# An attention and two-layer feed-forward kernel in which one softmax mask in sixteen goes to GpSimd, and the first keys are loaded ahead of tau

## The chip, the cores and the metric

The kernel runs on one core of a Trainium2 chip. The metric is the device time of one execution in microseconds (us). A core has a matmul engine (TensorE, in profiles PE, its weight loads PEld), VectorE (DVE), ScalarE (ACT), GpSimd (POOL) and SyncE (SP), which here only issues DMAs. Each engine runs its own instructions in order; semaphores tie the engines together.

## What is computed

The reference, cut to what matters. The attention output goes through two feed-forward blocks; q, k, v are (4, 8, 576, 64), tau is 0.02, the feed-forward blocks work on 2304 tokens of width 512 with 2048 hidden units.

```python
scores = scale * np.matmul(q, k.transpose(0, 1, 3, 2))
thresh = np.max(scores, axis=-1, keepdims=True) - tau
scores = np.where(scores >= thresh, scores, -1000000000.0)
scores = scores - np.max(scores, axis=-1, keepdims=True)
attn = np.exp(scores)
attn = attn / (np.sum(attn, axis=-1, keepdims=True) + 1e-09)
x = np.matmul(attn, v)             # heads put side by side: (2304, 512)
h = x @ w_in;  x = (h * (1.0 / (1.0 + np.exp(-1.702 * h)))) @ w_out
h = x @ w_in2; out = (h * np.tanh(np.log1p(np.exp(h)))) @ w_out2
```

So a softmax row keeps only the scores that lie within tau of the row's largest one.

## The kernel before, in words

**Attention stage.** The 4 x 8 heads are taken in 16 pairs. The 576 query rows of a pair make four "full" groups (128 rows of each of the two heads), and the last 64 rows of four heads make a "mix" group after every second pair: 64 + 8 = 72 groups, numbered gi = 0 to 71. A group's two halves (i = 0 and 1) each go through these steps:

- `qk` (L600): TensorE writes the scores into two PSUM tiles `sc`, four matmuls for a full group (L623).
- `softmax_a` (L632): VectorE scales the scores into an SBUF buffer (ring `ss`, which a profile shows under the name `win2a` of the memory that it borrows) and takes the row's extreme with it (L646); GpSimd adds tau to that extreme (L650, one column, tile `nm`); ScalarE makes the exponentials into a tile `p` (L653; in a profile `g0a` to `g3a`); VectorE zeroes those below the threshold and sums the rest, in one instruction of 577 columns (L656, a scalar_tensor_tensor with an accumulated sum).
- `turn` (L678): TensorE transposes `p` into PSUM banks `tb` 0 to 2 (L692, L697; nine instructions for a group), ScalarE copies them to SBUF (L712; in a profile `wout1a`, `wout2a`, and a short one in `g0a`, `g1a`).
- `product` (L720): for every second group TensorE multiplies with v into bank `tb` 3 (L735, ten instructions), ScalarE copies the result (L744). `product_mix` (L747, L760) does the same for mix groups. `finish` (L662) takes reciprocals of the sums.

Until the first transposes TensorE is filled with dummy transposes (`keep_warm`, L574).

**Feed-forward stages.** `weights` and `stage` bring weights through ScalarE, VectorE and GpSimd (`conv_w`, L409 to L423, and L476 to L499), `load_xs` the tokens; `hidden` (L848) makes the hidden units with a 7-product Strassen scheme (L862), `out1` and `out2` multiply them with the second weights (L937, L940, L982). Some of the weights' preparation is done by VectorE, ScalarE and GpSimd while the attention stage still runs.

**What sets the order.** Nothing is issued as the code is read. Every operation is recorded with `add` in a class `Order` (L75): its engine, an assumed duration, what it reads and writes, and a rank. `Order.run` then plays the operations against the assumed durations, picks on each engine the ready one of lowest rank, and issues them in that order. Operations marked `port=True` are planned so that VectorE and GpSimd don't run them at the same time. The table `NUDGE` moves the rank of single operations, which it names by their running number. The order of each engine is thus fixed when the program is built; on the chip each engine takes it in that order and waits where it must.

**Start.** `make_ident` (L787) builds the identity, issues the load of tau (L789) and sets constants, and VectorE works out two columns from tau (L798, L799). The keys and values of a head pair are loaded by `prep` (L593: L596 and L597).

## Time and profile before

| what | value |
|---|---|
| median of 2 runs | 1024.49 us (1024.36 to 1024.63) |
| profiled execution: its time | 1024.41 us |
| profiled execution: its span, first to last instruction or landed DMA | 1022.5 us |
| busy in the span: PE / DVE / ACT / POOL | 1016.1 / 829.7 / 659.1 / 166.0 us |
| granted TensorE clock, mean | 0.999 of full speed |

The span is the part that the trace shows; 1.9 us of the execution's time lie outside it. "Busy" is the union of an engine's instructions. An engine that is busy all the time need not set the time, and one that idles costs nothing unless another waits for it, so the waits and the start times are read beside the busy shares.

### The profile page before, as it was taken

The page shows a single profiled execution, that of the slowest core. Times are in us where ns is not written, and L with a number is a line of the kernel's source. Part 1 is how long each engine was busy: PE and PEld are TensorE (multiplying, and loading weights), DVE is VectorE, ACT ScalarE, POOL GpSimd, SP SyncE. Part 2 cuts the span into 40 slices and gives each one's busy share as a digit, 9 for nine tenths or more (in the row PEclk, how much of TensorE's full clock was granted, in tenths as well). Part 3 has the DMA queues.
Part 4 walks back from the last instruction along what each step waited for, and adds up shares of the span by engine and source line. Part 5 has one row for each costly group of instructions (what it writes and reads, how often), then busy time and mean ns, then how long its engine had stood idle before and what let it go on. Part 6 is the DMA issues. An engine that isn't in the chain of part 4 may idle for free.

```text
span 1022.5 us, 17345 instructions
## 1 busy us (share of the span) xinstructions
PE 1016.1 (99%) x6362; PEld 865.9 (85%) x6362; DVE 829.7 (81%) x1642; ACT 659.1 (64%) x1262; POOL 166.0 (16%) x182
## 2 busy tenths in 40 slices
PE   9999999999999999999999999999999999999998
PEld 6666666666899999999999999989989899889987
DVE  7999999999989898888888779865598575975643
ACT  5988888888976768766777667644464444544421
POOL 2333544323222211201121011000000000000000
PEclk9999999999999999999999999999999999999999
DMA  5443347432256538664475553511144211232001
GB/s 198 138 135 101 117 141 236 161 98 74 87 169 210 182 124 282 243 201 159 146 271 200 193 185 110 194 67 62 63 124 145 83 49 55 93 114 83 21 1 63
DMA packets 55366, 137.53 MB, mean 134 GB/s; under 512 B 8432, under 2 KB 18672, under 8 KB 55280
## 3 DMA queue, kind: packets, MB, share of 16 engines
q1 hardware_dynamic: 55280, 136.41, 39.7%
q8 instruction: 50, 0.82, 0.3%
q14 instruction: 36, 0.29, 0.1%
HBM read 105.38 MB, written 31.01 MB: 133 GB/s over the span
## 4 chain that ended last, share of the span: by engine, by line
PE 99%; DMA 0%; DVE 0%; ACT 0%; issue 0%; SPq 0%; ACTq 0%
PE h L862 34%; PE tb L982 13%; PE tb L937 13%; PE sc L623 8%; PE tb L735 8%; PE tb L697 7%; PE h L940 7%; PE h L982 6%; PE tb L692 1%; PE tb L760 1%; DMA win1a<-in_kq 0%; PE tb L574 0%; DVE x21b L1000 0%; ACT wout2a L712 0%; ACT wout1a L712 0%
## 5 line engine op out<-in xcount | busy, mean ns | idle before, releaser
L876 DVE TENSOR_TENSOR hs<-h,u 128x384 f32<-128x384 f32 x144 | 79.9, 555 | 82.5 <-PE h L862 44.9
L862 PE MATMUL h<-xq,win2b 128*128 128x384 f32 x672 | 131.2, 335 | 0.0
L862 PE MATMUL h<-xq,win 128*128 128x384 f32 x672 | 131.1, 336 | 0.0
L862 PE MATMUL h<-xq,win1b 128*128 128x384 f32 x672 | 131.0, 335 | 0.0
L884 ACT COPY u<-h 128x384 f32<-128x384 f32 x144 | 68.8, 478 | 83.6 <-PE h L862 82.7
L862 PEld LDWEIGHTS h<-xq,win2b 128*128 128x128 f32 x672 | 115.9, 188 | 5.4 <-ACT u L884 0.2
L862 PEld LDWEIGHTS h<-xq,win1b 128*128 128x128 f32 x672 | 116.0, 188 | 5.3
L862 PEld LDWEIGHTS h<-xq,win 128*128 128x128 f32 x672 | 115.5, 188 | 5.2 <-ACT u L884 0.3
L646 DVE TENSOR_SCALAR_CACHE_REDUCE win2a<-sc,nqsc 128x576 f32<-128x576 f32 x144 | 111.6, 810 | 5.1 <-PE sc L623 4.7
L879 ACT ACTIVATE hs<-hs 128x384 f32<-128x384 f32 x144 | 75.9, 527 | 60.4 <-DVE hs L876 59.3
L650 POOL TENSOR_SCALAR nm<-nm,tau_p 128x1 f32<-128x1 f32 x144 | 81.8, 569 | 160.8 <-DVE win2a L646 159.5
L623 PE MATMUL sc<-win1a 64*128 64x288 f32 (+3 forms) x672 | 89.9, 414 | 0.3 <-DMA win1a<-in_kq 0.3
L481 DVE TENSOR_TENSOR sv<-sv 128x256 f32<-128x256 f32 x192 | 82.2, 429 | 1.3
L421 POOL TENSOR_TENSOR sg<-sg,sr 128x1024 uint32<-128x1024 uint32 x16 | 40.9, 2558 | 213.9 <-DVE sg L418 94.4
L623 PEld LDWEIGHTS sc<-win1a 64*128 64x128 f32 (+1 forms) x672 | 50.6, 173 | 26.1 <-issue 8.3
L476 ACT CAST win1b<-sv 128x256 fp32r<-128x256 f32 (+1 forms) x96 | 42.2, 445 | 33.9 <-DVE sv L481 28.9
L476 ACT CAST win2b<-sv 128x256 fp32r<-128x256 f32 (+1 forms) x96 | 42.3, 443 | 33.0 <-DVE sv L481 24.6
L476 ACT CAST win<-sv 128x256 fp32r<-128x256 f32 (+1 forms) x96 | 42.2, 446 | 27.5 <-DVE sv L481 21.7
L477 DVE TENSOR_TENSOR win2b<-sv,win2b 128x256 fp32r<-128x256 f32 (+1 forms) x96 | 50.6, 532 | 9.8 <-ACT win2b L476 9.6
L421 POOL TENSOR_TENSOR sv<-sv,sr 128x1024 uint32<-128x1024 uint32 x16 | 42.7, 2671 | 78.7 <-DVE sv L418 27.3
L477 DVE TENSOR_TENSOR win1b<-sv,win1b 128x256 fp32r<-128x256 f32 (+1 forms) x96 | 45.6, 478 | 10.1 <-ACT win1b L476 9.9
L477 DVE TENSOR_TENSOR win<-sv,win 128x256 fp32r<-128x256 f32 (+1 forms) x96 | 46.3, 486 | 7.2 <-ACT win L476 6.9
(244 smaller groups left out, 2285.7 us busy)
## 6 DMA issues: line engine op xcount, KB each, us to landing
sv<-w_d SPq DMA_DIRECT2D x80, 512.0 KB
sr<-in_w_in SPq DMA_DIRECT2D x16, 1024.0 KB
sr<-in_w_out SPq DMA_DIRECT2D x32, 512.0 KB
win1a<-in_kq SPq DMA_DIRECT2D x16, 576.0 KB
xr<-x_d SPq DMA_DIRECT2D x24, 384.0 KB
w_d<-sv SPq DMA_DIRECT2D x16, 512.0 KB
w_d<-sg SPq DMA_DIRECT2D x16, 512.0 KB
x_d<-xo SPq DMA_DIRECT2D x16, 288.0 KB
```

What stands on the lines that cost most here:

```text
L421: lambda: nc.gpsimd.tensor_tensor(bits, bits, word(0), ALU.add), keys, [kval], rank, port=True)
L476: add("ACT", t_act(256 * m, psum=False), lambda: nc.scalar.copy(at(0), src), [ku] + pre_in, keys, rank)
L477: add("DVE", t_dve(256 * m), lambda: nc.vector.tensor_tensor(at(1), src, at(0), ALU.subtract), [ku], keys, rank, port=True)
L481: add("DVE", t_dve(256), lambda: nc.vector.tensor_tensor(out, x, y, op), [], [ku], rank, port=True)
L623: nc.tensor.matmul(sc[i][at:at + m, g, c0:c0 + n], kq2[rows, q0:q0 + m], kq2[rows, k0:k0 + n], start=True, stop=True)
L646: lambda: nc.vector.tensor_scalar(n3, s3, nqsc, None, ALU.mult, ALU.min, accum_out=nm[:, 0:1]),
L650: lambda: nc.gpsimd.tensor_scalar(nm[:, 1:2], nm[:, 0:1], tau_p, 0.0, ALU.add, ALU.add),
L735: nc.tensor.matmul(av[64 * i:64 * i + 64], vr[:, vc:vc + 64], p[:, a:a + 256], start=(c == 0), stop=(c == 4))
L862: nc.tensor.matmul(dst(), w[:, h, c], xq[p][:, x, cs], start=(start and i == 0), stop=(p in (5, 6) and i == 5), skip_group_check=True)
L876: add("DVE", t_dve(HALF), lambda: nc.vector.tensor_tensor(ht[:, cs], x(), y, ALU.add), [kx, ky], [kh + (j,)], rank - 4.0)
L937: nc.tensor.matmul(acc2[e](), w[:, x], g(y)[:, 0:512], start=first, stop=last, skip_group_check=True)
L982: nc.tensor.matmul(acc2[t](), g(x)[:, t * 128:(t + 1) * 128], w[:, y], start=(k == i == j == 0), stop=(k == KP - 1 and i == 1 and j == 2), ...
```

## The change

Four edits.

1. `softmax_a` has a new argument `shared`. It is true for half i = 1 of every eighth group (gi = 1, 9, ..., 65: nine of the 144 masks). There the VectorE instruction with mask and sum is replaced by three: GpSimd compares the scores with the threshold into a buffer `le` (tensor_scalar, 576 columns), GpSimd multiplies the exponentials by it in place (tensor_tensor, 576 columns), and ScalarE copies the 577 columns back over the scores' buffer only to accumulate their sum. The `le` buffers are the four `hs` tiles, which the attention stage doesn't use otherwise.
2. The load of tau leaves `make_ident` and is issued in `prep` right behind the first load of keys.
3. The two VectorE instructions on tau become an operation of their own, `make_tau`.
4. `NUDGE` is another table (some 640 entries for 290), since the running numbers of the operations have moved and the order was chosen anew.

```diff
+MASK = 8
 NUDGE = {
-    13: -39, 28: 13, 31: 1, 65: 13, 68: 135, 85: 31, 100: 46, 114: -1, 119: 25, 134: 39, 153: 63,
...
+    2: 20, 4: 20, 15: -27, 19: -18, 32: 62, 36: 5, 44: 4, 45: -118, 49: -12, 50: -5, 51: -5, 54: 20,
...
+    les = Ring([t[:, 0:S] for t in hss.tiles], "hs", 4)
...
         dma(lambda: nc.sync.dma_start(out=kq2, in_=kq[b, hp]), 589824, w=[kkq], rank=rank)
+        if not head:
+            dma(lambda: nc.sync.dma_start(out=tau_b, in_=tau.to_broadcast([128, 1])), 512, w=["tau"], rank=rank)
+            add("DVE", 0.25, make_tau, ["tau"], ["qsc"], -4.0)
         dma(lambda: nc.sync.dma_start(out=vr, in_=v[b, hp]), 393216, w=[kvr], rank=rank)
...
-    def softmax_a(sums, ksum, col, rank, bank, pair, i):
+    def softmax_a(sums, ksum, col, rank, bank, pair, i, shared):
...
+        if shared:
+            le, kle = les.next()
+            add("POOL", t_ts(S),
+                lambda: nc.gpsimd.tensor_scalar(le, ns[:, 4:4 + S], nm[:, 1:2], 1.0, ALU.is_le, ALU.mult),
+                [kns, kn + (1,)], [kle], rank, port=True)
+            add("POOL", 0.16 + S * 2.3e-3,
+                lambda: nc.gpsimd.tensor_tensor(p[:, at:at + S], le, p[:, at:at + S], ALU.mult),
+                [kle], [kp], rank, port=True)
+            add("ACT", t_act(S + 1, psum=False) + 0.2,
+                lambda: nc.scalar.activation(
+                    ns[:, 3 + i:4 + S + i], p[:, whole], AF.Copy, accum_out=sums[:, col:col + 1]),
+                [kp, "qsc"], [kns, ksum + (col,)], rank)
+            return kp
...
     def make_ident():
         make_identity(nc, ident)
-        nc.sync.dma_start(out=tau_b, in_=tau.to_broadcast([128, 1]))
...
+    def make_tau():
         nc.vector.tensor_scalar_max(tau_p, tau_b, 0.0)
         nc.vector.tensor_scalar(nqsc, tau_b, 0.0, -scale, ALU.is_ge, ALU.mult)
...
-                ps.append(softmax_a(sums, ksum, col, gi, bank, (pair, kpair), i))
+                ps.append(softmax_a(sums, ksum, col, gi, bank, (pair, kpair), i, i == 1 and gi % MASK == 1))
```

In the built program the lines have moved: L596 has become L626, L597 L630, L623 L656, L653 L686, L692 L738, L697 L743, L712 L758, and the new ScalarE sum is L697. Three places of the new order follow.

SP at the start of the program. Before (`win1a` is the memory that holds the keys, `x20a` and its like the values):

```order
L789 DMA tau_b<-in_tau 128x1
L596 DMA win1a<-in_kq 128x1152
L597 DMA x20a<-in_v 128x768
L596 DMA win1a<-in_kq 128x1152
L597 DMA x21a<-in_v 128x768
```

And now:

```order
L626 DMA win1a<-in_kq 128x1152
L628 DMA tau_b<-in_tau 128x1
L630 DMA x20a<-in_v 128x768
L626 DMA win1a<-in_kq 128x1152
L630 DMA x21a<-in_v 128x768
```

The first keys and tau have changed places.

ACT in the first groups, from the exponentials of group 1 (`g1a`) to the copies of its transposes (`tb_74`, `tb_75`, `tb_76` are the banks `tb` 0, 1 and 2). Before:

```order
L653 ACTIVATE g1a<-win2a,nm_132 128x576
L653 ACTIVATE g1a<-win2a,nm_133 128x576
L712 COPY wout1a<-tb_74 128x4x128
L712 COPY wout1a<-tb_75 128x4x128
L712 COPY g0a<-tb_76 128x128
L653 ACTIVATE g2a<-win2a,nm_134 128x576
L653 ACTIVATE g2a<-win2a,nm_135 128x576
L712 COPY wout1a<-tb_74 128x4x128
L712 COPY wout1a<-tb_75 128x4x128
```

And now:

```order
L686 ACTIVATE g1a<-win2a,nm_132 128x576
L686 ACTIVATE g1a<-win2a,nm_133 128x576
L758 COPY wout1a<-tb_74 128x4x128
L758 COPY g0a<-tb_76 128x128
L758 COPY wout1a<-tb_75 128x4x128
L686 ACTIVATE g2a<-win2a,nm_134 128x576
L697 ACTIVATE win2a,sm_138<-g1a 128x577
L686 ACTIVATE g2a<-win2a,nm_135 128x576
L758 COPY wout1a<-tb_74 128x4x128
L758 COPY wout1a<-tb_75 128x4x128
```

The sum over the masked half of group 1 stands between the two exponentials of group 2, ahead of the copies of group 1's transposes.

PE some 25 us into the program, around the scores of the group 6 (`sc_81`, `sc_82`); `g3a` and the `g0a` and `g1a` behind it are the groups 3, 4 and 5. Before:

```order
L697 MATMUL tb_74<-ident,g0a 128x128 x4
L697 MATMUL tb_75<-ident,g2a 128x128 x4
L623 MATMUL sc_81<-win1a 128x288
L623 MATMUL sc_82<-win1a 128x288
L623 MATMUL sc_81<-win1a 128x288
L623 MATMUL sc_82<-win1a 128x288
L697 MATMUL tb_75<-ident,g3a 128x128 x4
L692 MATMUL tb_76<-ident,g0a 128x128
L697 MATMUL tb_75<-ident,g0a 128x128 x4
```

And now:

```order
L743 MATMUL tb_75<-ident,g2a 128x128 x4
L743 MATMUL tb_74<-ident,g0a 128x128 x4
L656 MATMUL sc_81<-win1a 128x288
L656 MATMUL sc_82<-win1a 128x288
L656 MATMUL sc_81<-win1a 128x288
L656 MATMUL sc_82<-win1a 128x288
L743 MATMUL tb_75<-ident,g3a 128x128 x4
L738 MATMUL tb_76<-ident,g0a 128x128
L743 MATMUL tb_74<-ident,g1a 128x128 x4
L743 MATMUL tb_75<-ident,g0a 128x128 x4
```

Four transposes of group 5 now stand between the two uses of bank `tb_75`.

## Rows read from the trace of the kernel before

**Rows 1.** The page: busy time, and the chain that ended last.

```profile
PE 1016.1 (99%) x6362; PEld 865.9 (85%) x6362; DVE 829.7 (81%) x1642; ACT 659.1 (64%) x1262; POOL 166.0 (16%) x182
...
PE 99%; DMA 0%; DVE 0%; ACT 0%; issue 0%; SPq 0%; ACTq 0%
```

**Rows 2.** Waits of PE but the first: line, releaser: us in total, times, longest.

```profile
PE tb L697 <- ACT wout2a L712: 1.0, 1, 1.0
PE sc L623 <- DMA win1a<-in_kq: 0.3, 1, 0.3
```

**Rows 3.** Busy time by stage (columns: length, PE, PEld, DVE, ACT, POOL, clock, DMA).

```profile
9.00:264.00 255.00, 253.88 (x2219) 168.14 (x2216) 251.25 (x645) 214.97 (x429) 97.78 (x148) 1.00 0.42 135
264.00:1022.50 758.50, 754.87 (x4100) 691.39 (x4099) 575.45 (x970) 441.49 (x833) 66.91 (x26) 1.00 0.39 133
```

**Rows 4.** Timeline of PE in mid attention (start, length, what).

```profile
105.63 1.04 PE L697 MATMUL tb<-ident,g2a 128*128 128x128 f32 x8
106.50 0.27 PE L692 MATMUL tb<-ident,g2a 128*128 128x128 f32 x1
...
109.76 1.09 PE L697 MATMUL tb<-ident,g3a 128*128 128x128 f32 x8
110.78 0.69 PE L760 MATMUL tb<-wout1a,x21a 128*64 128x64 f32 x16
```

**Rows 5.** The chain that ended last, in order of time, in the second layer.

```profile
871.93 2.08 PE h L862 x12
...
876.77 1.06 PE h L862 x6
```

**Rows 6.** Timeline of the start.

```profile
0.74 0.38 SPq L789 DMA_DIRECT2D tau_b<-in_tau  x1
1.17 0.42 SPq L596 DMA_DIRECT2D win1a<-in_kq  x1
1.36 3.78 PE L574 MATMUL tb<-ident 128*128 128x128 f32 x20 [1.36 <-POOL ident masks.py:199]
...
3.63 0.15 DVE L798 TENSOR_SCALAR tau_p<-tau_b 128x1 f32<-128x1 f32 x1 [2.11 <-DMA tau_b<-in_tau]
...
5.47 1.24 PE L623 MATMUL sc<-win1a 64*128 64x288 f32 x8 [0.34 <-DMA win1a<-in_kq]
...
6.75 0.82 DVE L646 TENSOR_SCALAR_CACHE_REDUCE win2a<-sc,nqsc 128x576 f32<-128x576 f32 x1 [2.90 <-PE sc L623]
```

**Rows 7.** Timeline around the mask of group 1.

```profile
10.62 0.29 POOL L650 TENSOR_SCALAR nm<-nm,tau_p 128x1 f32<-128x1 f32 x1 [1.93 <-DVE win2a L646]
...
11.36 0.80 POOL L650 TENSOR_SCALAR nm<-nm,tau_p 128x1 f32<-128x1 f32 x1 [0.45 <-DVE win2a L646]
...
13.69 1.82 PE L623 MATMUL sc<-win1a 64*128 64x288 f32 x8
...
14.15 0.81 DVE L656 SCALAR_TENSOR_TENSOR g1a<-win2a,nm,g1a 128x577 f32<-128x577 f32 x1
...
14.37 1.46 ACT L653 ACTIVATE g2a<-win2a,nm 128x576 f32<-128x576 f32 x2
...
15.44 1.10 PE L697 MATMUL tb<-ident,g1a 128*128 128x128 f32 x8
...
16.14 1.07 ACT L712 COPY wout1a<-tb 128x512 f32<-128x512 f32 x2 [0.31 <-PE tb L697]
...
16.78 0.63 PEld L735 LDWEIGHTS tb<-wout1a,x20a 128*64 128x64 f32 x8 [0.36 <-ACT wout1a L712]
```

**Rows 8.** Timeline at 26 us: GpSimd's long instruction, and PE's longest wait.

```profile
26.03 2.41 POOL L421 TENSOR_TENSOR sv<-sv,sr 128x1024 uint32<-128x1024 uint32 x1 [0.71 <-ACT wout1a L712]
...
26.36 0.82 DVE L646 TENSOR_SCALAR_CACHE_REDUCE win2a<-sc,nqsc 128x576 f32<-128x576 f32 x1 [0.47 <-PE sc L623]
...
27.85 1.21 DVE L656 SCALAR_TENSOR_TENSOR g1a<-win2a,nm,g1a 128x577 f32<-128x577 f32 x1
...
28.00 0.66 PE L697 MATMUL tb<-ident,g0a 128*128 128x128 f32 x4 [0.97 <-ACT wout2a L712]
```

76 rows, old and new, of the table NUDGE are left out of this document.

## The prediction

> **What bounds the kernel now.** I read the page first. TensorE is busy 99% of the span, and the chain that ended last is TensorE's for 99% too [rows 1]. The ends of matmuls are modelled, so a busy PE alone proves little; the waits and the distances between starts decide. In the list of PE's waits only two stand behind the wait for the identity: 0.3 us for the first keys and 1.0 us for a PSUM bank that ScalarE had not copied yet [rows 2]. Starts show the same. In mid attention eight transposes take 0.87 us from their first start to the next instruction, 0.109 each, and eight others take 1.02 us to the start of another kind of matmul: 0.87 and 0.15 for the turn [rows 4]. That pattern repeats through the stage; only in the first 30 us do pieces take clearly longer than their like (below). So TensorE is truly the bound, at full clock [rows 3], and there is little waiting left to take away.
>
> By stage, VectorE looks like a second bound: 251.25 of 255 us busy in the attention stage [rows 3]. But it also prepares weights and tokens there that are due only in the feed-forward stages, where it is busy for 575 of 758 us, and PE almost never waits for it. VectorE's time is worth something only where a PE instruction stands behind it.
>
> **The change part by part.**
>
> *What VectorE loses.* Nine masks of 0.81 us (one stands in [rows 7]): 7.3 us. PE doesn't wait for masks in mid attention, so I cost this at nothing; the freed time goes to preparation of weights. What hides it is PE's own 255 us of matmuls.
>
> *PE's own work.* The matmuls are the same in number and shape. The new order has 86 unbroken runs of transposes for 84: two more turns of 0.15 us [rows 4], +0.30. Two of the 16 mix products (L760) get other neighbours, which may change a turn each; I take -0.15, one turn of the two. In the feed-forward stages the runs of hidden and output matmuls fall from 500 to 466, but a turn costs nearly nothing there: twelve matmuls of L862 in one run take 2.08 us, 0.173 each, and six with a turn behind them 1.06, 0.177 each [rows 5]. Sum: +0.15 us.
>
> *Keys ahead of tau.* The first scores start at 5.47 when their keys land, which were issued at 1.17, 0.43 us behind tau's load at 0.74 [rows 6]. Issued at 0.74 they land by 5.0. PE is then still in its 20 dummy transposes: they end at 1.36 + 3.78 = 5.14, and the next kind can start some 0.07 before a modelled end, so at 5.07. Gain 0.40 us. The price is tau. It is now issued near 1.17 behind 576 KB of keys. Before, VectorE got it 2.9 us after the issue (3.63 less 0.74) [rows 6]. With the same delay it comes at 4.1, and right behind the keys at about 5.2; with two VectorE instructions of 0.15 the scale column is ready by 5.5. The first reader is L646, at 6.75 before and 6.35 now. That leaves 0.8 us at the worst of these; if tau even waited for the values' 384 KB, some 1.5 us more, up to 0.7 us of the start would be lost again. I take -0.40.
>
> *The mask on GpSimd and ScalarE.* The trace has neither GpSimd instruction at 576 columns. For the compare the ends are 0.29 (L650 with one column [rows 7]) and 1.36 (two inputs, L421's 2.41 x 576/1024 [rows 8]); I take 0.8, VectorE's time for the same width. For the multiply I take 1.36, the nearest row in kind; its ends are 0.8 and 2.4 (L421 unscaled). ScalarE's sum costs 0.78 like an exponential (half of 1.46 or so [rows 7]), and up to 0.2 for reading the accumulator. I follow the first of the nine, in the old clock. Group 1's threshold is ready at 12.16, compare to 12.96, multiply to about 14.3, or 14.9 if it must first wait for a VectorE mask as that L650 did (0.80 for 0.29). The VectorE mask that it replaces ended at 14.96 [rows 7]. So the transposes of group 1 at 15.44 are not late. But ScalarE now has the sum between the two exponentials of group 2: the first ends at 15.1, the sum runs to 15.95, the second exponential to 16.7, and only then comes the copy of group 1's transposes, at 16.14 before. ScalarE idled 0.31 before that copy [rows 7], so the copy is 0.86 - 0.31 = 0.55 late. The next PE instruction, L735 at 16.78, waited for just that copy [rows 7]: PE loses 0.55 us. With ends from 0 (sum and multiply both short) to 1.4 (the pair 0.85 slower). The eight later shares meet a deeper pipeline: ScalarE is busy 215 of 255 us and PE runs a group or two behind the masks; I cost them at nothing, with 0.55 each as the other end.
>
> One rule of the Trainium skill speaks against the change: the page "Perfetto Trace Analysis", section "Optimizing Scalar/DVE Operations", says that GpSimd and VectorE share an SBUF read port, so that moving work between the two might not help. The trace agrees in part: beside L421 a mask took 1.21 instead of 0.81 us, but L646, which reads PSUM, ran at its usual 0.82 [rows 8]. By that rule each share holds up the masks for some 2.2 us to save 0.81; it is the third rival. The page "GPSIMD Engine Reference", section "4.1 Engine selection", puts a two-input GpSimd operation at about twice VectorE's time, and one input near line rate; by that the pair would be an estimated 0.8 + 1.6 us, a quarter more than I took, and the first share's loss 0.55 to 0.8.
>
> *The wait at 26 us.* PE lost 0.97 us there, waiting for ScalarE to free a bank between two uses of it [rows 8]. In the new order four transposes (0.44) stand between these uses, but ScalarE has a weight preparation of 1024 columns ahead of that copy in place of two exponentials of 576. Ends: all of it gone (-0.97) and, if ScalarE gets there later, 0.3 more; I take -0.4, the time of the work put between.
>
> Sum against the profiled execution: 1024.41 - 0.40 + 0.15 + 0.55 - 0.40 = 1024.3 us. That execution lies 0.08 under the median of 1024.49; the difference is less than I can work out.
>
> **The rivals.**
>
> *The early waits go.* The planner has more freedom, and PE's waits at 13.69 (this L623 lasts 1.82 us, the first one 1.24: 0.58), at 15.44 (1.34 us to L735, where nine transposes and a turn make 9 x 0.109 + 0.15 = 1.13: 0.2) and at 26 us (0.97) all vanish [rows 4, 6 to 8]. 1024.41 - 0.40 + 0.15 - 1.75 = 1022.4. This is nearly the floor, as nothing else waits. For: VectorE has 0.8 us less by the third group. Against: the VectorE order up to that point is unchanged, and the sum on ScalarE is in the way.
>
> *Slower: ScalarE's in-order wait repeats.* Each of the nine sums waits at the head of ScalarE's queue for GpSimd's multiply, and the PSUM copies behind it come 0.55 or more late; PE waits for each. This decides wherever ScalarE's idle time ahead of such a copy is under 0.86 us. Three shares in the first 100 us: 1024.41 - 0.25 + 3 x 0.55 = 1025.8; all nine 1029.1. For: the first share shows it. Against: ScalarE idles 40 us in the stage.
>
> *Slower: the port.* Masks wait 2.2 us for each pair, net of 0.81 saved 1.4 us by nine, 12.6 us of VectorE, which has only 3.75 free in the stage [rows 3]. If preparation can't give way, PE is held up for 9 us: 1033. Against: the preparation can wait, and L646 isn't held.
>
> *The change does nothing where it says so:* VectorE's 7.3 us buy nothing at all and only the start counts. That is my forecast with the other terms at nothing, 1024.0 to 1024.2.
>
> **How the numbers follow.** My forecast, with that last case, 0.68 (its own range 1023.3 to 1025.6); early waits gone 0.13; ScalarE's wait repeated 0.16; the port 0.03. The range 1022.3 to 1027.0 holds the first two and the milder half of the third. A measurement of this kernel can tell about 2% from no change, 20.5 us. No case comes near it on the fast side, since PE's work is fixed; on the slow side it would take over 2 us of PE waiting for each share. So 0.01 for faster, 0.97 for the same, 0.02 for slower.
>
> **What would show it.** PE's first scores at 5.07; L646 still right behind them; the copies of group 1's transposes half a microsecond late against PE, and PE's list of waits still about 2 us. PE busy within 1 us of 1016. If PE waits near each ScalarE sum, the third case is right; if VectorE's masks last over 1 us beside the new GpSimd pair and PE waits for them, the port. A first L646 later than 6.4 would mean that tau came late.

## The result, and the profile after

The changed kernel takes 1039.12 us (median of 2 runs, 1038.60 to 1039.64) against 1024.49: 1.0139 of before, 95% interval 1.0122 to 1.0156. That is 14.6 us slower, outside the predicted range of 1022.3 to 1027.0.

The page of the changed kernel: busy time, and the chain that ended last.

```profile
PE 1024.7 (99%) x6362; PEld 869.9 (84%) x6362; DVE 832.7 (80%) x1624; ACT 666.0 (64%) x1280; POOL 199.6 (19%) x200
...
PE 89%; DVE 4%; ACT 3%; POOL 2%; issue 1%; POOLq 0%; DVEq 0%; ACTq 0%
```

The busy share of PE is 99% as before [rows 1] and says nothing: a matmul that waits inside a run counts as busy (8.6 us more for the same 6362 matmuls). The chain does say something: PE had all of it, now 9% of the span hangs on VectorE, ScalarE and GpSimd. VectorE is not less busy than before, though it makes nine masks of 0.81 us fewer, so other instructions of it must have become longer.

By stage. The attention stage is cut at 278 us now, as the last products of both kernels lie 14 us apart (columns as in [rows 3]):

```profile
9.00:278.00 269.00, 261.94 (x2221) 171.72 (x2221) 254.48 (x627) 222.30 (x445) 131.18 (x167) 1.00 0.42 132
278.00:1036.80 758.80, 755.10 (x4101) 691.52 (x4099) 575.70 (x968) 441.66 (x834) 67.46 (x26) 1.00 0.39 132
```

The feed-forward stages are as long as in [rows 3], 758.8 us for 758.5; the attention stage has the whole loss, 269 us for 255. GpSimd is busy for 33 us more there. To place the loss I added up, over PE's starts, how much longer each run of like matmuls took to the next one than such a run usually takes in before. That comes to 3.0 us in before and 17.2 here, nearly all of it in the first 240 us: 14.2 us more, the measured loss.

The two GpSimd operations, by groups (count, busy us, mean ns, idle before):

```profile
L691 POOL TENSOR_SCALAR hs<-win2a,nm 128x576 f32<-128x576 f32 x9 | 22.6, 2513 | 0.8
L694 POOL TENSOR_TENSOR g1a<-hs,g1a 128x576 f32<-128x576 f32 x9 | 14.4, 1601 | 0.7
```

The multiply is about what I took (1.36). The compare takes 2.51 us on average, three times the 0.8. What that does, in the timeline around the mask of group 1 (it answers to [rows 7]):

```profile
12.85 2.59 POOL L691 TENSOR_SCALAR hs<-win2a,nm 128x576 f32<-128x576 f32 x1
...
15.53 1.40 POOL L694 TENSOR_TENSOR g1a<-hs,g1a 128x576 f32<-128x576 f32 x1
...
16.90 0.56 POOL L683 TENSOR_SCALAR nm<-nm,tau_p 128x1 f32<-128x1 f32 x2
16.96 0.69 ACT L697 ACTIVATE win2a<-g1a 128x577 f32<-128x577 f32 x1 [1.19 <-POOL g1a L694]
16.98 0.75 PEld L743 LDWEIGHTS tb<-ident,g1a 128*128 128x128 f32 x7 [0.80 <-POOL g1a L694]
...
17.24 0.82 DVE L702 SCALAR_TENSOR_TENSOR g2a<-win2a,nm,g2a 128x577 f32<-128x577 f32 x1 [2.42 <-POOL nm L683]
...
18.92 0.63 PEld L781 LDWEIGHTS tb<-wout1a,x20a 128*64 128x64 f32 x8 [1.09 <-ACT wout1a L758]
```

Three engines wait for the pair here. PE's transposes of group 1 start at 16.98 for the multiply, ScalarE's sum at 16.96, and VectorE stands idle for 2.42 us: the threshold of group 2, one column wide, is queued on GpSimd behind compare and multiply. The lists of waits of VectorE and ScalarE (up to 270 us) show that this goes on:

```profile
DVE g2a L702 <- POOL nm L683: 8.6, 6, 2.4
```

```profile
ACT win2a L697 <- POOL g1a L694: 8.1, 7, 1.6
```

And PE's own list:

```profile
PE tb L743 <- ACT wout2a L758: 1.9, 5, 0.6
PE sc L656 <- DVE win2a L679: 1.5, 1, 1.5
...
PE tb L743 <- POOL g1a L694: 1.1, 3, 0.6
PE tb L781 <- ACT wout1a L758: 1.1, 2, 0.9
```

Against two waits of 1.3 us in all [rows 2] these are more, but no single one is large, and it is not plain from them which of the three waits matters. One line points elsewhere: the 1.5 us for a scale of VectorE. Its place in the timeline:

```profile
142.30 0.69 DVE L447 TENSOR_SCALAR sv<-sv 128x1024 uint32<-128x1024 uint32 x1
...
143.07 2.39 POOL L450 TENSOR_TENSOR sv<-sv,sr 128x1024 uint32<-128x1024 uint32 x1
143.10 2.99 DVE L702 SCALAR_TENSOR_TENSOR g3a<-win2a,nm,g3a 128x577 f32<-128x577 f32 x1
...
146.88 1.97 PE L656 MATMUL sc<-win1a 64*128 64x288 f32 x8 [1.49 <-DVE win2a L679]
```

No masked half is near. A mask starts 0.03 us behind GpSimd's add of weight preparation (L421 before), and takes 2.99 us instead of 0.81. Before, the worst was 1.48. So there are two suspects besides the waits: the order, and the port.

The start, which answers to [rows 6]:

```profile
0.74 0.39 SPq L626 DMA_DIRECT2D win1a<-in_kq  x1
...
1.36 4.53 PE L603 MATMUL tb<-ident 128*128 128x128 f32 x20 [1.36 <-POOL ident masks.py:199]
...
5.82 1.48 PE L656 MATMUL sc<-win1a 64*128 64x288 f32 x8
6.62 0.15 DVE L845 TENSOR_SCALAR tau_p<-tau_b 128x1 f32<-128x1 f32 x1 [5.10 <-DMA tau_b<-in_tau]
```

The keys are issued 0.43 us earlier, but PE takes their scores 0.35 us later: the dummy transposes ahead of them took 4.53 us for 3.78. By their starts this is TensorE's clock. In before they stand 0.21 us apart up to 4.0 us and 0.11 apart from 4.3 us on; in the changed kernel all twenty stand 0.21 apart, as at the lower of the two clock levels (1.2 for 2.4 GHz). The trace's first record of the granted clock begins at 4.21 in before and at 6.36 here; ahead of it a profile shows 1.00 only because it has no record.

### The profile page after: what moved, and what is told of

It reads as the page before. It is cut to its first block, busy times and chain, and to the rows that moved or that the text cites. A ratio compares the mean times of both kernels' runs of the same rounds, so it can differ in the third digit from the quotient of the medians.

```text
span 1036.8 us, 17241 instructions
## 1 busy us (share of the span) xinstructions
PE 1024.7 (99%) x6362; PEld 869.9 (84%) x6362; DVE 832.7 (80%) x1624; ACT 666.0 (64%) x1280; POOL 199.6 (19%) x200
## 4 chain that ended last, share of the span: by engine, by line
PE 89%; DVE 4%; ACT 3%; POOL 2%; issue 1%; POOLq 0%; DVEq 0%; ACTq 0%
PE h L909 33%; PE tb L1029 13%; PE tb L984 12%; PE h L1029 6%; PE sc L656 6%; PE h L987 6%; PE tb L781 6%; PE tb L743 5%; POOL hs L691 1%; POOL g1a L694 1%; PE tb L806 1%; PE tb L738 1%; DVE win2a L679 1%; DVE xq L581 1%; PE tb L603 1%
## 5 line engine op out<-in xcount | busy, mean ns | idle before, releaser
L683 POOL TENSOR_SCALAR nm<-nm,tau_p 128x1 f32<-128x1 f32 x144 | 79.5, 555 | 141.0 <-DVE win2a L679 139.6
L656 PE MATMUL sc<-win1a 64*128 64x288 f32 (+3 forms) x672 | 95.0, 415 | 1.5 <-DVE win2a L679 1.5
L510 DVE TENSOR_TENSOR sv<-sv 128x256 f32<-128x256 f32 x192 | 86.4, 451 | 1.3
L450 POOL TENSOR_TENSOR sg<-sg,sr 128x1024 uint32<-128x1024 uint32 x16 | 41.2, 2576 | 213.2 <-ACT sr L440 80.0
L656 PEld LDWEIGHTS sc<-win1a 64*128 64x128 f32 (+1 forms) x672 | 53.8, 174 | 27.6 <-DVE win2a L679 9.8
L450 POOL TENSOR_TENSOR sv<-sv,sr 128x1024 uint32<-128x1024 uint32 x16 | 41.7, 2605 | 75.9 <-DVE sv L447 46.3
L506 DVE TENSOR_TENSOR win2b<-sv,win2b 128x256 fp32r<-128x256 f32 (+1 forms) x96 | 47.0, 491 | 7.9 <-ACT win2b L505 7.7
```

The costliest lines, as they stand in the source:

```text
L450: lambda: nc.gpsimd.tensor_tensor(bits, bits, word(0), ALU.add), keys, [kval], rank, port=True)
L506: add("DVE", t_dve(256 * m), lambda: nc.vector.tensor_tensor(at(1), src, at(0), ALU.subtract), [ku], keys, rank, port=True)
L510: add("DVE", t_dve(256), lambda: nc.vector.tensor_tensor(out, x, y, op), [], [ku], rank, port=True)
L656: nc.tensor.matmul(sc[i][at:at + m, g, c0:c0 + n], kq2[rows, q0:q0 + m], kq2[rows, k0:k0 + n], start=True, stop=True)
L683: lambda: nc.gpsimd.tensor_scalar(nm[:, 1:2], nm[:, 0:1], tau_p, 0.0, ALU.add, ALU.add),
```

## The experiments

Times are medians; the ratio, with its 95% interval, is to before, run on the same chip. "PE's lost time" is the sum told of above: 3.0 us in before, 17.2 in the changed kernel.

### Keys ahead of tau, alone

e1 is the kernel before with only the order of these two loads changed.

```diff
+        def load_keys():
...
+            if first_of_all:
+                nc.sync.dma_start(out=tau_b, in_=tau.to_broadcast([128, 1]))
...
-        nc.sync.dma_start(out=tau_b, in_=tau.to_broadcast([128, 1]))
```

> The kernel before, with one thing of the change: the first keys are issued ahead of tau (and the two VectorE instructions on tau follow); all other instructions stand as before. Theory A (the loss of 14.6 us is made by the nine GpSimd masks): within 1 us of before, 1023.9 to 1025.1; my forecast said -0.4. Theory C (the start is what loses: in the changed kernel the first scores came 0.35 us and the second ones 0.60 us later than before): +0.6 us or more, 1025.1 and up. The profile tells whether the first dummy transposes run slow for longer than before, and when tau arrives.

Measured: 1024.93 us, 0.9999 (0.9990 to 1.0008). Nothing is gained. In e1's trace the first scores start at 5.30, and the 20 dummies took 4.01 us. Their length differs from one execution to the next by more than the gain looked for: e5 and e16 below, which start as before does, took 4.53. And the earlier scores are not used earlier:

```profile
6.39 0.15 DVE L602 TENSOR_SCALAR tau_p<-tau_b 128x1 f32<-128x1 f32 x1 [4.88 <-DMA tau_b<-in_tau]
...
6.74 0.82 DVE L655 TENSOR_SCALAR_CACHE_REDUCE win2a<-sc,nqsc 128x576 f32<-128x576 f32 x1
```

The first scale starts at 6.74, as in before (6.75 [rows 6]), since it waits for the column worked out from tau.

### The order, with and without the nine masks

e2 takes the changed kernel's order and gives the nine masks back to VectorE, at the multiply's place. e8 leaves compare, multiply and sum out (nine shares are neither masked nor summed). e16 leaves the same nine masks out of the kernel before. e12 is e8 with one VectorE shift of weight preparation (L447) put behind the mask that follows it, near 135 us.

```diff
e2, at the multiply's place
-                lambda: nc.gpsimd.tensor_tensor(p[:, at:at + S], le, p[:, at:at + S], ALU.mult),
+                lambda: nc.vector.scalar_tensor_tensor(
...
e8, three times, this is the first (e16 does the same at the mask of a shared half)
-                lambda: nc.gpsimd.tensor_scalar(le, ns[:, 4:4 + S], nm[:, 1:2], 1.0, ALU.is_le, ALU.mult),
+                lambda: None,
e12, after planning
+        early = sorted(self.shifts, key=dve.index)[5]
+        behind = dve[dve.index(early) + 1]
...
```

> The changed kernel with its own order on every engine, but the nine masks are done by VectorE again: the two GpSimd instructions and ScalarE's sum are left away, and the VectorE instruction with mask and sum stands where the GpSimd multiply was planned. Theory A (the loss comes from the GpSimd masks): the PE waits go, 1024 to 1026 us. Theory B (the new order is worse in itself, whoever makes the masks): 1035 us or more. Theory C (the start): at most 1 us of the loss stays.

> The changed kernel with its own order, and nothing in place of the nine masks: compare, multiply and sum are left out (those nine halves are not masked, and their sums stay 1). Theory B (the new order loses 7 us in itself, whatever the masks cost): 1030 to 1032. Rival (the new order is good once the nine masks are off VectorE and the other engines are not late): 1024 to 1025.5.

> The kernel without the nine masks (1028.7 us), with one pair of VectorE instructions exchanged: near 135 us a mask (normally 0.81 us) took 3.04 because GpSimd's 1024-column addition had begun 0.02 us ahead of it; the shift that releases this addition now stands behind the mask. If the shared port made these 2.2 us, and PE's 1.9 us of waiting behind them, the mask takes 0.8 us again and the time falls by 1 to 2 us, to 1026.7 to 1027.7. If not, it stays at 1028.7.

> The kernel before with the nine masks (and their sums) left out and nothing in their place: the most that the idea could give in that order, with GpSimd and ScalarE doing the work for nothing. Theory 'VectorE's 7.3 us are worth nothing, since PE waits for masks almost nowhere': 1022.7 to 1025 us, ratio 0.9985 to 1.0005. Rival 'VectorE is the second bound of the attention stage, its time counts in full or half': 1017 to 1021 us, ratio 0.993 to 0.9965. Against e8 (the new order with the same left out, 1.0040) it tells what the new order itself costs.

Measured: e2 1031.96 us, 1.0071 (1.0059 to 1.0084); e8 1028.69, 1.0040 (1.0026 to 1.0054); e12 1027.59, 1.0028 (1.0019 to 1.0037); e16 1026.46, 1.0018 (1.0009 to 1.0027).

e2 and e8 both lie between the outcomes that I had expected. So the new order costs about 4 us before GpSimd does anything, and it costs them with less work to do; with the nine masks on VectorE (e2) it costs 7.3. e16 is the surprise, above both of its ranges: the old order with nine masks *less* is slower than with them. The timeline of e16 shows why:

```profile
100.54 0.68 DVE L418 TENSOR_SCALAR sv<-sv 128x1024 uint32<-128x1024 uint32 x1
101.33 3.05 DVE L656 SCALAR_TENSOR_TENSOR g2a<-win2a,nm,g2a 128x577 f32<-128x577 f32 x1
101.36 2.40 POOL L421 TENSOR_TENSOR sv<-sv,sr 128x1024 uint32<-128x1024 uint32 x1
...
105.18 1.49 PE L623 MATMUL sc<-win1a 64*128 64x288 f32 x6 [0.87 <-DVE win2a L646]
```

And the same place in before, not shown so far:

```profile
101.37 0.80 DVE L656 SCALAR_TENSOR_TENSOR g2a<-win2a,nm,g2a 128x577 f32<-128x577 f32 x1
...
101.59 2.85 POOL L421 TENSOR_TENSOR sv<-sv,sr 128x1024 uint32<-128x1024 uint32 x1 [0.68 <-DVE sv L418]
```

In before a mask of group 1's kind stands ahead of the shift L418. GpSimd's add waits for that shift and meets the next mask 0.22 us after its start: the mask takes 0.80 and the add 2.85. Without the earlier mask the two start together, and now the mask is held until the add ends, and is done 0.6 us behind it: 3.05. PE loses 0.9 us at the next scores. Both kernels have the same two instructions; 0.2 us decide who waits. e8 has the same collision near 135 us, and e12 takes it away:

```profile
135.68 3.04 DVE L701 SCALAR_TENSOR_TENSOR g3a<-win2a,nm,g3a 128x577 f32<-128x577 f32 x1
135.70 2.39 POOL L450 TENSOR_TENSOR sv<-sv,sr 128x1024 uint32<-128x1024 uint32 x1
...
139.52 1.97 PE L656 MATMUL sc<-win1a 64*128 64x288 f32 x8 [1.10 <-DVE win2a L679]
```

```profile
135.29 0.82 DVE L710 SCALAR_TENSOR_TENSOR g3a<-win2a,nm,g3a 128x577 f32<-128x577 f32 x1 [0.25 <-ACT g3a L695]
...
138.43 1.24 PE L665 MATMUL sc<-win1a 64*128 64x288 f32 x8
```

The first fence is e8, the second e12. PE's lost time falls from 7.3 to 5.3 us; the ratios fall by 0.0012, but their intervals overlap. About half of what e12 keeps over before are waits in runs of 9 to 14 transposes (0.82 us at 26, 0.84 at 50, in e8, over 0.109 for each and 0.15 for the turn; PE's list of waits has them for bank copies), which are longer in the new order: in before no such run has more than 10, now four have 13 or 14. The one at 26 us is shorter than in before, where it is 1.20 by the same count, but not gone. The other half was not separated.

### The compare's speed

e3 turns the compare into an add, e4 drops its second operation. e5 is the *old* order with the nine masks on GpSimd (the compare right behind the threshold, the multiply at the mask's place, ScalarE's sum after the group's last copy, one of the nine too late for its reciprocal); e6 is e5 with the add. In e3 and e6 the nine shares are thus multiplied by a sum of score and threshold.

```diff
e3 and e6
-                lambda: nc.gpsimd.tensor_scalar(le, ns[:, 4:4 + S], nm[:, 1:2], 1.0, ALU.is_le, ALU.mult),
+                lambda: nc.gpsimd.tensor_scalar(le, ns[:, 4:4 + S], nm[:, 1:2], 1.0, ALU.add, ALU.mult),
e4, in the compare's place
+                lambda: nc.gpsimd.tensor_scalar(le, ns[:, 4:4 + S], nm[:, 1:2], None, ALU.is_le),
e5
-            lambda: nc.vector.scalar_tensor_tensor(
+            multiply if shared else lambda: nc.vector.scalar_tensor_tensor(
```

> The changed kernel with the GpSimd compare replaced by an addition of the same operands, shapes and place (is_le becomes add), so nine halves are multiplied by a sum and not masked: part of the computation is changed. It asks what made that instruction 2.59 us long. If the comparison itself is slow, the instruction takes 0.6 to 0.9 us, as the planner assumed, and by theory A the time falls to 1025 to 1028 us. If any GpSimd tensor_scalar of 576 columns takes that long, it stays at 2.2 to 2.6 us and the time at 1038 to 1040.

> The changed kernel with the GpSimd compare in one operation (is_le alone, without the multiplication by 1.0 behind it); the result is the same. If the second operation is what costs, the instruction falls from 2.59 to about 1.3 us or less and by theory A the time to about 1031 us (half of the excess of the compare over the planned 0.72 us goes). If the comparison itself is slow, it stays over 2 us and the time within 2 us of 1039.

> The kernel before, with its own order on every engine, and the nine masks by GpSimd and ScalarE: the compare behind the threshold of the same half, the multiply where VectorE's mask stood, the sum behind the last copy of the group's transposes. With masks on VectorE the new order ran 7.1 us over before, and with the GpSimd masks 14.6. If the two parts simply add (theory D: 7 us for the order, 7 for the long GpSimd pair), this one takes about 1032 us. If the pair costs mainly in the new order, whose slack is used up (theory E), it takes 1025 to 1028.

> The same as the run before it (order of the kernel before, nine masks on GpSimd), with the comparison replaced by an addition, which took 1.10 us for 2.59; nine halves are then scaled and not masked. Theories D and E both expect the pair to cost little now: 1024.5 to 1026. If it stays near the run before it, the length of the compare is not what costs.

Measured: e3 1031.67 us, 1.0062 (1.0048 to 1.0076); e4 1037.19, 1.0113 (1.0098 to 1.0129); e5 1041.01, 1.0160 (1.0146 to 1.0174); e6 1033.18, 1.0080 (1.0067 to 1.0094). The operation itself, by groups, in e3 and then in e4:

```profile
L691 POOL TENSOR_SCALAR hs<-win2a,nm 128x576 f32<-128x576 f32 x9 | 9.2, 1026 | 0.8
```

```profile
L691 POOL TENSOR_SCALAR hs<-win2a,nm 128x576 f32<-128x576 f32 x9 | 18.2, 2022 | 0.8
```

A compare 1.5 us shorter, nine times, gives back 7.9 us in the new order and 8.2 in the old one (by the ratios). So about half of the loss is the compare's length, in either order. e5 is 9 us over the slower outcome that I had expected for it; e3 and e6 are 4 and 7 us over what I had expected with a short compare. How the length gets to PE was still open. In the old order waits are what goes with it: VectorE waits 9.0 us for thresholds in e5 and 1.2 in e6, and PE itself waits for the multiply in e5 and not in e6:

```profile
PE tb L713 <- POOL g1a L659: 4.5, 5, 1.4
```

### Taking the waits away

e7 gives the thresholds of the groups behind a masked half to VectorE. In e9 the multiply writes a buffer of its own, so nobody waits for the pair's result (the nine shares stay unmasked). e10 does both. e11 is the changed kernel planned with 2.3 us for the compare instead of the 0.72 that the planner assumed, with the table of nudges as it is.

```diff
e7
-            lambda: nc.gpsimd.tensor_scalar(nm[:, 1:2], nm[:, 0:1], tau_p, 0.0, ALU.add, ALU.add),
+            lambda: (nc.vector if after_shared else nc.gpsimd).tensor_scalar(
...
e9
-                lambda: nc.gpsimd.tensor_tensor(p[:, at:at + S], le, p[:, at:at + S], ALU.mult),
+                lambda: nc.gpsimd.tensor_tensor(le, le, p[:, at:at + S], ALU.mult),
e11
-            add("POOL", t_ts(S),
+            add("POOL", 2.3,
```

> The changed kernel, but the thresholds (one column) of the group behind each masked one are made by VectorE, in the place where GpSimd's were planned, so that no threshold stands behind the GpSimd pair. If the thresholds queued behind the pair make the second half of the loss (VectorE waited 9.2 us for them in seven places), the time falls to 1032 to 1034. If it is PE and ScalarE waiting for the masked half itself (ScalarE's sums waited 8.1 us for the multiply), it stays above 1036.

> The changed kernel with all its instructions in their places, but the GpSimd multiply writes into its own buffer and not into the exponentials: so neither the transposes on PE nor ScalarE's sum wait for the GpSimd pair (nine halves are not masked), while the pair still takes its time on GpSimd, still holds the port, and the thresholds still stand behind it. If PE and ScalarE waiting for the masked half is the main part of the 10.4 us that the nine masks cost in this order, 1030 to 1032 us. If the thresholds behind the pair are, 1036 to 1038.

> The run before it, and the thresholds of the group behind each masked one made by VectorE: the pair is awaited by nobody, and what is left of it is GpSimd's time and the port that it shares with VectorE. If waiting for results is all that it costs, about 1029 us, as with the masks left out (1028.7). If the port costs by itself (VectorE's masks held up by the pair), 1031 us or more.

> The changed kernel, correct, with one number of the planner changed: it is told 2.3 us for the compare, as measured without delay, and not 0.72, so it orders all engines anew (with the same table of nudges, which was made for the other order). If the loss is only that the plan was made with a wrong duration, 1026 to 1030 us. If the pair costs whatever the order, because the next thresholds must wait for it or the masked half comes late, 1034 us or more.

Measured: e7 1037.12 us, 1.0125 (1.0111 to 1.0139); e9 1039.19, 1.0144 (1.0129 to 1.0160); e10 1037.67, 1.0127 (1.0113 to 1.0141); e11 1043.07, 1.0178 (1.0164 to 1.0192).

The waits in which I had put the loss can go, and most of the loss stays. e9, slower than either outcome expected: that PE and ScalarE wait for the multiply costs nothing measurable in this order. e7 and e10: that VectorE no longer waits for thresholds brings 1 to 2 us. Planning with the true duration (e11) makes another order, and a worse one; as its nudges were chosen for the other, it doesn't rule out an order that would hide the pair. The trace of e10 shows what came in the waits' place:

```profile
103.19 2.59 POOL L692 TENSOR_SCALAR hs<-win2a,nm 128x576 f32<-128x576 f32 x1
...
105.87 1.79 POOL L695 TENSOR_TENSOR hs<-hs,g1a 128x576 f32<-128x576 f32 x1
...
106.32 1.95 DVE L703 SCALAR_TENSOR_TENSOR g2a<-win2a,nm,g2a 128x577 f32<-128x577 f32 x1
...
108.45 0.75 DVE L679 TENSOR_SCALAR_CACHE_REDUCE win2a<-sc,nqsc 128x576 f32<-128x576 f32 x1
...
109.27 0.51 PE L656 MATMUL sc<-win1a 64*128 64x288 f32 x1 [0.69 <-DVE win2a L679]
```

The next mask, no longer late, now runs into the multiply: 1.95 us for 0.81. The scale behind it is late, and PE's scores wait 0.69 us. Of e10's nine multiplies eight stretch a VectorE instruction like this, by 7.8 us in all. Masks and multiply are both marked `port=True`, so the plan keeps them apart, but it does so with 0.72 us for the compare.

### The port

Three variants of e10. e13 leaves the multiply out, e14 the compare (the multiply then runs at its place), e15 makes the second operation one with a single input. All three leave the nine shares unmasked.

```diff
e13
-                lambda: nc.gpsimd.tensor_tensor(le, le, p[:, at:at + S], ALU.mult),
+                lambda: None,
e14, and no compare
+                lambda: nc.gpsimd.tensor_tensor(le, ns[:, 4:4 + S], p[:, at:at + S], ALU.mult),
e15
+                lambda: nc.gpsimd.tensor_scalar(le, le, 1.0, 0.0, ALU.add, ALU.add),
```

> e10_neither (nobody waits for GpSimd's pair; thresholds of the groups behind it on VectorE) with the multiply left out too: compare and ScalarE's sum remain, so the nine shares are summed unmasked. Theory 'the slow compare pushes the multiply to where VectorE does its own two-input work, and one of the two is held up': the multiply's eight collisions (7.8 us of stretched VectorE work in e10) are gone, and the compare's own (two of 0.4) stay; a ratio of 1.004 to 1.0075 (1029 to 1032 us). Rival 'GpSimd is busy too long, whatever it does': the compare, 2.6 of the 4.0 us of a pair, is still there; 1.009 to 1.012. Rival 'ScalarE's sum of 0.87 us': as now, 1.011 to 1.013.

> e10_neither with the compare left out: GpSimd only multiplies (scores by probabilities, into a buffer of its own), so the nine shares are summed unmasked. The multiply now starts where the compare did, beside VectorE's scales of the next two groups, which read PSUM. Theory of the collisions: few stretches of VectorE by the multiply (0 to 3 of 9), ratio 1.004 to 1.0075. Rival 'the multiply costs wherever it lies': the stretches stay at 6 to 8 and the ratio at 1.010 to 1.013.

> e10_neither with the multiply replaced by a one-input operation (compare's output plus 1.0 plus 0.0, in place): the shares are summed unmasked as there. Theory that the second input from SBUF makes the collisions: the second operation (about 0.75 to 1.1 us) lies where the multiply lay, but holds VectorE little (under 0.45 us each), ratio 1.004 to 1.008. Rival 'any GpSimd operation there does': eight stretches of 0.5 to 1.1 us, ratio 1.009 to 1.013.

Measured: e13 1030.91 us, 1.0060 (1.0045 to 1.0075); e14 1031.75, 1.0065 (1.0048 to 1.0082); e15 1033.24, 1.0083 (1.0068 to 1.0098). In the timeline of e13, at the place shown of e10:

```profile
101.15 2.59 POOL L692 TENSOR_SCALAR hs<-win2a,nm 128x576 f32<-128x576 f32 x1
...
104.47 0.82 DVE L703 SCALAR_TENSOR_TENSOR g2a<-win2a,nm,g2a 128x577 f32<-128x577 f32 x1
...
106.39 1.86 PE L656 MATMUL sc<-win1a 64*128 64x288 f32 x8
```

The compare is as long as it was, the mask has its 0.82, PE doesn't wait. In e14:

```profile
100.64 1.58 POOL L695 TENSOR_TENSOR hs<-win2a,g1a 128x576 f32<-128x576 f32 x1
...
101.77 0.82 DVE L679 TENSOR_SCALAR_CACHE_REDUCE win2a<-sc,nqsc 128x576 f32<-128x576 f32 x1 [0.61 <-PE sc L656]
...
103.98 0.82 DVE L703 SCALAR_TENSOR_TENSOR g2a<-win2a,nm,g2a 128x577 f32<-128x577 f32 x1
```

The multiply, 2.6 us earlier, lies beside scales, which read PSUM, and is over when the next mask comes. So neither operation costs by itself what the pair costs in e10; the pair costs some 6 us more because the slow compare pushes the multiply to where VectorE does its own two-input work. e15 is the sharper test, as its second operation keeps GpSimd busy longer than the multiply did (mean 2.34 us for 1.57 in e10; I had expected 0.75 to 1.1):

```profile
105.28 2.53 POOL L695 TENSOR_SCALAR hs<-hs 128x576 f32<-128x576 f32 x1
...
105.70 1.22 DVE L703 SCALAR_TENSOR_TENSOR g2a<-win2a,nm,g2a 128x577 f32<-128x577 f32 x1
```

The mask is held for 0.4 us, not 1.1, and e15 is 4.5 us faster than e10 by the ratios. It missed my ratio of at most 1.008 by a little, probably because one more collision of L450 with a mask came in (7.2 us of stretch by L450 instead of 4.7). So GpSimd's time as such doesn't explain what e10 loses.

The table puts the runs side by side. "Over before" is the ratio less 1, times 1024.5 us. "Waits" is VectorE waiting for thresholds (its list of waits); "stretch" sums what VectorE's instructions took over the usual for their line and shape (where over 0.12 us) beside GpSimd's second operation (how often) and beside its weight add. The last column is the time that TensorE's granted clock stood at 0.50 inside the profiled execution.

| run | over before, us | waits | stretch: second operation | stretch: weight add | clock at 0.50, us |
|---|---|---|---|---|---|
| before | 0 | 0.2 | none | 1.2 | none |
| changed kernel | 14.2 | 9.2 | 3.5 (3) | 5.0 | none |
| e9 | 14.8 | 8.8 | 3.5 (3) | 5.0 | 3.4 |
| e10 | 13.0 | 0.6 | 7.8 (8) | 4.7 | 3.4 |
| e7 | 12.8 | 0.6 | 7.5 (8) | 4.9 | none |
| e4 | 11.6 | 5.0 | 5.2 (5) | 4.7 | 6.8 |
| e15 | 8.5 | 0.8 | 2.3 (7) | 7.2 | none |
| e14 | 6.7 | 1.0 | 0.4 (1) | 4.7 | 3.4 |
| e3 | 6.4 | 1.0 | 0.6 (1) | 4.8 | 3.4 |
| e13 | 6.1 | 1.0 | none | 4.8 | 3.4 |
| e8 | 4.1 | 1.0 | none | 4.8 | none |
| e5 (old order) | 16.4 | 9.0 | 3.9 (4) | 3.4 | 3.4 |
| e6 (old order) | 8.2 | 1.2 | 3.7 (4) | 3.4 | 3.4 |

Waits and stretches replace each other: a VectorE that waits for a late threshold is not there to be held by the multiply, and the other way round. That is why taking away one of them bought 1 to 2 us only. In the old order the multiply stretches as much with the fast compare as with the slow one; the two differ in waits.

The last column is a loss that I had not looked for. In these runs of the new order the clock falls to its lower level (1.2 GHz) just behind PE's longest wait, that of 1.49 us at 146.88 in the changed kernel, for the scale behind the mask that L450 held. In e13 (length, PE, clock, DMA; then the products that follow):

```profile
143.20:146.50 3.30, 3.30 (x18) 0.50 0.01 3
```

```profile
142.77 3.35 PE L782 MATMUL tb<-wout1a,x21a 128*64 128x256 f32 x16
```

In the changed kernel, whose clock stayed up in the profiled execution, the same products:

```profile
148.79 1.95 PE L781 MATMUL tb<-wout1a,x21a 128*64 128x256 f32 x16
```

PE loses 1.4 us by it. It doesn't happen in every execution: e13's four took 1029.73 and 1030.25 us with a mean granted clock of 0.999 and 1.000, and 1031.57 and 1031.70 with 0.998. e14 has one with 1.000 (1030.19) and e3 one (1029.56); e8 and e12 have none under 0.999. e10's four, all with 0.998, are still 6 us over the two of e13 with 0.998, so the readings above stand. What decides whether the clock falls behind such a wait stays open.

## Why the prediction was wrong

*What bounds the kernel.* Right for before, and PE's work stayed the same. The conclusion from it, that VectorE's time counts only where PE stands behind it, hid the rule that failed: VectorE is 98.5% busy in the stage [rows 3], so a microsecond that it *loses* can come through to PE a group later (e10: 1.1 us of stretch, 0.69 us of PE's wait). What it *gains* depends on the order: nothing in the old one (e16, which has one collision more), 3.1 us for nine masks in the new one (e2 less e8).

*The mask on GpSimd: the step that failed.* "I take 0.8" for the compare; it took 2.23 us at its shortest, and 2.59 in the seven of nine places where a VectorE mask had started 0.32 us ahead of it. My upper end, 1.36, came from the nearest row in kind and was too low as well. The multiply (1.40 at its shortest, 1.60 on average) and the sum (0.69 plus 0.19 for the accumulator) were right. For the first share I forecast the copies 0.55 us late, with PE waiting for them; PE's product at 18.92 waited for such a copy, but the whole stretch was already late, and by e9 this chain isn't what costs in the new order.

*"The eight later shares meet a deeper pipeline: I cost them at nothing."* Wrong, and the costlier half of the step: the nine shares cost 10.1 us (14.2 less e8's 4.1), not 0.55. I followed the pair's result only. I didn't follow GpSimd's own queue (the thresholds behind the pair) nor ask where the multiply lies against VectorE's two-input instructions. With the compare fast, the multiply beside scales, this value would have been nearly right: e3, e13 and e14 cost 2 to 2.6 us over e8, all nine shares together, and 0.9 to 1.6 us over e8's median in the four of their executions with a mean clock of 0.999 or 1.000. What is left then was not separated; ScalarE's sum is in all three. A fast compare alone isn't enough: e6, where the multiply stands at the mask's place, is 8.2 us over before.

*VectorE's 7.3 us at nothing.* About right for the old order, but the end below nothing was missing: e16 loses 1.8 us by the same work left out.

*The port, 0.03.* The mechanism was there, with its price of 9 us, and I set it aside because "the preparation can wait, and L646 isn't held". L646's successor indeed isn't held (no scale took over 0.82 us in any run). But preparation can't wait: the order on VectorE is fixed, and a stretched instruction delays all behind it. In the changed kernel the port is the smaller part, 3.5 us of stretch beside the multiply against 9.2 us of waiting for thresholds behind the pair, which no rival had. The Trainium skill's page "Perfetto Trace Analysis", section "Optimizing Scalar/DVE Operations", had the rule that spoke against the change: GpSimd and VectorE share an SBUF read port, so moving work between them might not help. The runs bear it out, with 10.1 us lost by nine masks moved. The Trainium skill's page "SBUF — State Buffer", section "SBUF: two separate sides", is more exact: of a VectorE operation with two SBUF inputs and a GpSimd operation that reads SBUF, whichever starts first has the shared ports for its whole length. The two-input GpSimd rows agree in how long the mask is held: in e16 and e10 it ends 0.6 us behind the add or multiply beside it. But in e16 the mask is the one held, although its reported start is 0.03 us ahead. The one-input rows don't agree: in the changed kernel a mask at 195.44 was done in 1.22 us, inside a compare that ran from 195.31 to 197.54.

*Keys ahead of tau, -0.40.* Not there (e1). The step took the dummies' length as fixed at 3.78 us; it was 4.01 in e1 and 4.53 in the changed kernel, as the clock rose later. And tau, taken at 4.1 to 5.2, came later: its first reader ran at 6.39 in e1 and 6.62 in the changed kernel, near the worst case named (5.2 plus some 1.5). In the changed kernel the first scale didn't wait for it, as the scores were late too. Where they weren't it did: in e12, with dummies of 3.76 us, scores start at 5.05 as forecast, and the first scale at 6.78, no earlier than in before.

*PE's turns +0.15 and the wait at 26 us -0.40.* The wait fell as forecast, from 1.20 us by the count above to 0.82 in e8 and 0.79 in the changed kernel. But there was no term for what a new order does to collisions and bank copies elsewhere. e8 puts the order at 4.1 us in all.

The sum that the runs give in place of mine: about 4 us for the new order (1.2 of it one collision of the weight add, by ratios with overlapping intervals), 2 us for the pair and the sum in a harmless place (about half of it the fallen clock), 8 us because the slow compare moves the multiply and the thresholds into VectorE's way: 14 of the measured 14.2 to 14.6. Of the 4 us some half stays unexplained, and the 8 us are not split between waits and stretches.

## What to carry to other kernels

Before work goes from VectorE to GpSimd, look up the operation in a trace, not the engine's usual rate: one compare was three times as slow as an add of the same shape, and two additions in place (e15) were nearly as slow as the compare. Then lay the new instructions beside VectorE's two-input ones and beside what waits in GpSimd's own queue; both engines run in order, so a held instruction delays everything behind it. And when a wait is removed and the time stays, list the lengths of the instructions that used to wait: the loss has often moved into them.

## What was not expected of the hardware

- GpSimd at 128 x 576 fp32, the shortest of nine: compare and multiply-by-one 2.23 us, compare alone 1.74 (e4), add and multiply-by-one 0.75 (e3), two adds of constants in place 2.16 (e15). Which operation it is matters three times; why was not tried.
- A VectorE mask beside GpSimd's weight add ends 0.6 us behind it if it starts 0.03 us before or behind it (2.99 to 3.05 us for 0.81), and is not held when it starts 0.22 us ahead (0.80). Beside a one-input operation it is held 0.2 to 0.4 us, and the slow one holds no longer than the fast one: a mask that starts 0.13 us behind it takes 1.22 us beside the compare of 2.23 us and beside e3's add of 0.75.
- Leaving work out can make a kernel slower (e16, 1.0018).
- The 20 dummy transposes at the start took 3.78, 4.01 and 4.53 us in three traces. The first record of the clock begins at 4.21, 4.69 and 6.36 us, and the dummies stand 0.21 us apart until then and 0.11 behind it; what makes the clock rise sooner or later stays open.
- After a wait of PE of 1.1 to 1.5 us the granted clock fell to 0.50 in six profiled executions (e3, e4, e9, e10, e13, e14), and after the same wait stayed at 1.00 in those of the changed kernel, e2, e7, e8 and e15. In e5, e6 and e11 it fell elsewhere, at 112, 109 and 20 us.
